# A gated mix of a spectral filter and an S5 state-space layer: FFT kept in SBUF, chunked recurrence kept in SBUF, transposes by DMA

## The chip, the cores and the metric

One Trainium2 chip, one core of it. The metric is the device time of one execution in microseconds (us). The engines are TensorE (PE, matmuls into PSUM; its weight loads are listed as PEld), VectorE (DVE), ScalarE (ACT), GpSimd (POOL) and SyncE (SP, which here only issues DMAs).

## What is computed

The input x has 2048 tokens of 1024 channels, in bf16. Two branches read it and a gate per token mixes them:

```python
def reference(A_x, A_w_r, A_w_i, B_x, ..., gate_w):
    x = A_x
    g = sigmoid((x * gate_w).sum(-1, keepdims=True))
    # A: real 2-D FFT over tokens and channels, times a filter, back
    X = rfft2(x.astype(float32)) * (A_w_r + 1j * A_w_i)     # 2048 x 513
    a = irfft2(X, s=(2048, 1024)).astype(bfloat16)
    # B: complex diagonal recurrence over the tokens, 1024 states
    Lam_bar = exp(dt * Lam);  B_bar = ((Lam_bar - 1) / Lam)[:, None] * (B_re + 1j * B_im)
    Bu = x @ B_bar.T
    for t in range(2048):
        h = Lam_bar * h + Bu[t]
    b = 2 * real(hs @ (C_re + 1j * C_im).T) + x * Dskip
    return g * a + (1 - g) * b
```

## The kernel before

**Start.** x is loaded by SP in 16 blocks of 128 tokens (L160) into the space that C will take later. PE transposes every block in 8 pieces of 128 x 128 against an identity (helper `pe_transpose_block`, L149; the copy out of PSUM is L150) to xT, channels on partitions. DVE forms the gate's sums (L165). A few dozen tiny operations on 128 x 8 tiles make the per-state constants.

**Spectral branch** (`gfnet`, a generator). The token index is split as 128 x 16 (16 times s1 plus s2). For every residue j: the channel DFT as 16 matmuls of 512 columns against a dense cosine and sine matrix (`fd`, L346), then the 128-point token DFT with twiddles (L358 to L361). The result goes to DRAM (L365) and is read back with tokens in another order, a corner turn (`s2w`, L446); a 16-point DFT over the residues follows (L452 to L455), the product with the filter W on DVE (L459 to L464), the inverse 128-point DFT (L476 to L479), a second turn through DRAM (L482, read back at L497), the inverse 16-point DFT (`is2`, L500 and L502, 256 columns each), and the inverse channel DFT (L518, 16 matmuls of 512 per block). ACT copies every result out of PSUM. The finished branch, times the gate, goes to DRAM (ga_scratch). Columns 0 and 512 of the spectrum are handled by a fix-up of small operations (`fixup`).

**Recurrence** (`pass1`, for each of 8 blocks of 128 states). B's block is loaded (L284) and transposed by PE. Tables of cosine and sine over 512 steps are made on ACT and DVE (L287 to L300, with the helper `sincos`, L226 to L235). Then for 4 chunks of 512 tokens: 16 matmuls (L309), copy to SBUF on ACT (L312), rotation into the frame that turns with the state (L314, L316, L318, bf16 on DVE), two real scans (L321), and the carry for the next chunk (L326 to L330). Chunk 0 is rotated back at once (`rotate_out`, L275 to L278); chunks 1 to 3 are stored to DRAM in the rotating frame (L337), and the tables as well.

**Order.** The main loop runs `pass1(jb)`, transposes two blocks of C, and pulls the spectral generator on by a budget of hand-given costs; the rest of the generator follows the last block. The framework's scheduler then orders the instructions of each engine: an instruction that is ready may be placed ahead of one that still waits for a buffer. A DMA belongs to the queue of the engine that issues it (SP for nearly all, POOL for the constants that are cast).

**Output.** The chunks are read back from DRAM (L562, and L547 for chunk 0), rotated back by DVE (L275 to L278), and for each of 16 token tiles 32 matmuls of 512 columns form the product with C (L580); DVE adds the skip term and the spectral branch (L588, L590, L593) and SP stores the tile (L595).

Of the kernel before, what the change touches and what calls it, by code (L numbers as in the profile page):

```python
# [19 lines left out]
S = 2048  # L20
D = 1024
K = 512
NP = 1024
# [3 lines left out]

MAGIC = 12582912.0
INV2PI = float(1.0 / (2.0 * np.pi))
CW1 = 6.28125  # L30
CW2 = float(2.0 * np.pi - 6.28125)
PI_LO = float(np.nextafter(np.float32(np.pi), np.float32(0.0)))
HALF_PI = float(np.pi / 2)

DEBUG = {}


def _host_consts():
    d = np.arange(D)[:, None]
    k = np.arange(K)[None, :]  # L40
    ang = 2 * np.pi * ((d * k) % D) / D
    G = np.zeros((D, 2 * K))
    G[:, :K] = np.cos(ang)
    G[:, K:] = -np.sin(ang)
    G[:, K] = (-1.0) ** np.arange(D)
    kk = np.arange(K)[:, None]
    n = np.arange(D)[None, :]
    angi = 2 * np.pi * ((kk * n) % D) / D
    ck = np.full((K, 1), 2.0)
    ck[0] = 1.0  # L50
    Ginv = np.zeros((2 * K, D))
    Ginv[:K, :] = ck * np.cos(angi)
    Ginv[K:, :] = -2.0 * np.sin(angi)
    Ginv[K, :] = (-1.0) ** np.arange(D)
    Ginv /= float(D * S)
    s1 = np.arange(P)[:, None, None]
    s2 = np.arange(16)[None, :, None]
    m1 = np.arange(P)[None, None, :]
    angT = 2 * np.pi * (((16 * s1 + s2) * m1) % S) / S
    Tc, Ts = np.cos(angT), np.sin(angT)  # L60
    p = np.arange(P)
    q = p // 8
    a = p % 8
    angK = 2 * np.pi * ((q[:, None] * q[None, :]) % 16) / 16
    delta = (a[:, None] == a[None, :]).astype(np.float64)
    Kc, Ks = delta * np.cos(angK), delta * np.sin(angK)
    J = np.zeros((P, P))
    J[np.arange(P), 127 - np.arange(P)] = 1.0
    P0 = np.zeros((P, P))
    P0[(128 - np.arange(P)) % 128, np.arange(P)] = 1.0  # L70
    f32 = lambda z: np.ascontiguousarray(z, dtype=np.float32)
    return dict(
        G=np.ascontiguousarray(G.astype(np.float32).astype(ml_dtypes.bfloat16)), Ginv=f32(Ginv),
        T3=f32(np.stack([Tc, Ts, -Ts], axis=0).transpose(2, 1, 0, 3)),
        K3=f32(np.stack([Kc, Ks, -Ks], axis=0)),
        R12=f32(np.stack([np.concatenate([Kc, Ks], 1), np.concatenate([-Ks, Kc], 1)], 0)),
        JP=f32(np.stack([J, P0], axis=0)),
    )
# [3 lines left out]
def kernel(  # L82
# [22 lines left out]
    cG = nc.inline_tensor(hc["G"], name="c_G").ap()  # L105
    cGinv = nc.inline_tensor(hc["Ginv"], name="c_Ginv").ap()
    cT3 = nc.inline_tensor(hc["T3"], name="c_T3").ap()
    cK3 = nc.inline_tensor(hc["K3"], name="c_K3").ap()
    cR12 = nc.inline_tensor(hc["R12"], name="c_R12").ap()
    cJP = nc.inline_tensor(hc["JP"], name="c_JP").ap()  # L110

    dram = ctx.enter_context(tc.tile_pool(name="dram", bufs=1, space=DRAM))
    ga_dram = dram.tile([S, D], BF16, name="ga_scratch")
    turn1_dram = dram.tile([16, P, 2, K], BF16, name="turn1_scratch")
    turn2_dram = dram.tile([16, P, 2, K], BF16, name="turn2_scratch")
    col0_dram = dram.tile([P, 16, 2], BF16, name="col0_scratch")
    h_dram = dram.tile([NCH, P, 8, 2, TC], BF16, name="h_scratch")
    tab2_dram = dram.tile([P, 8, 3, TC], BF16, name="tab2_scratch")
    g_dram = dram.tile([S], FP32, name="g_scratch")
    ccol_dram = dram.tile([P, 16, 2], BF16, name="ccol_scratch")  # L120

    cpool = ctx.enter_context(tc.tile_pool(name="cpool", bufs=1))
    xpool = ctx.enter_context(tc.tile_pool(name="xpool", bufs=1))
    ctpool = ctx.enter_context(tc.tile_pool(name="ctpool", bufs=1))
    h0p = ctx.enter_context(tc.tile_pool(name="h0p", bufs=1))

    actx = ExitStack()
    gconst = actx.enter_context(tc.tile_pool(name="gconst", bufs=1))
    gt = actx.enter_context(tc.tile_pool(name="gt", bufs=3))
    wp = actx.enter_context(tc.tile_pool(name="wp", bufs=3))  # L130
    wt = actx.enter_context(tc.tile_pool(name="wt", bufs=1))
    fx = actx.enter_context(tc.tile_pool(name="fx", bufs=1))
    p1 = actx.enter_context(tc.tile_pool(name="p1", bufs=2))
    p1t = actx.enter_context(tc.tile_pool(name="p1t", bufs=1))
    up = actx.enter_context(tc.tile_pool(name="up", bufs=3))
    rp = actx.enter_context(tc.tile_pool(name="rp", bufs=1))
    hp = actx.enter_context(tc.tile_pool(name="hp", bufs=3))
    cp = actx.enter_context(tc.tile_pool(name="cp", bufs=2))
    stg = actx.enter_context(tc.tile_pool(name="stg", bufs=3))
    psA = actx.enter_context(tc.tile_pool(name="psA", bufs=2, space=PSUM))  # L140
    psU = actx.enter_context(tc.tile_pool(name="psU", bufs=2, space=PSUM))

    ident = cpool.tile([P, P], BF16, name="ident")
    make_identity(nc, ident)

    def pe_transpose_block(src_ap, dst_ap, evac):
        pt = psU.tile([P, 8, P], BF16, name="pt", tag="psu")
        for j8 in range(8):
            nc.tensor.transpose(out=pt[:, j8, :], in_=src_ap[:, P * j8:P * (j8 + 1)], identity=ident)  # L149
        evac(out=dst_ap, in_=pt)  # L150

    CT = [ctpool.tile([P, 8, D], BF16, name=f"CT{ri}") for ri in range(2)]
    xT = xpool.tile([P, 8, S], BF16, name="xT")
    xT_A = xT.rearrange("p d (a b) -> p d b a", b=16)
    gw_bc = cpool.tile([P, D], BF16, name="gw_bc")
    nc.scalar.dma_start(out=gw_bc, in_=gate_w.partition_broadcast(P))
    glog = cpool.tile([P, 16], FP32, name="glog")
    for r in range(16):
        xn = CT[r // 8][:, r % 8, :]
        nc.sync.dma_start(out=xn, in_=x[P * r:P * (r + 1), :])  # L160
    for r in range(16):
        xn = CT[r // 8][:, r % 8, :]
        pe_transpose_block(xn, xT[:, :, P * r:P * (r + 1)], nc.vector.tensor_copy)
        gjunk = stg.tile([P, D], BF16, name="gjunk", tag="stg")
        nc.vector.scalar_tensor_tensor(out=gjunk, in0=xn, scalar=1.0, in1=gw_bc, op0=ALU.mult, op1=ALU.mult,  # L165
                                       accum_out=glog[:, r:r + 1])

    G_sb = gconst.tile([P, 8, 2 * K], BF16, name="G_sb", tag="G")
    cG_v = cG.rearrange("(j p) k -> p j k", p=P)
    for h in range(2):  # L170
        nc.sync.dma_start(out=G_sb[:, :, K * h:K * (h + 1)], in_=cG_v[:, :, K * h:K * (h + 1)])
    T3_sb = gconst.tile([P, 16, 3, P], BF16, name="T3_sb")
    nc.gpsimd.tensor_copy(out=T3_sb[:, 0, 0, 0:1], in_=xT[:, 7, S - 1:S])
    cT3_v = cT3.rearrange("j p t m -> p j t m")
    for q4 in range(4):
        nc.gpsimd.dma_start(out=T3_sb[:, 4 * q4:4 * (q4 + 1)], in_=cT3_v[:, 4 * q4:4 * (q4 + 1)])
# [162 lines left out]
    def gfnet():  # L339
# [13 lines left out]
        for j in range(16):  # L353
            X1 = X1_next
            if j + 1 < 16:
                X1_next = fd(j + 1)
# [269 lines left out]
```

## Time and profile before

| | |
|---|---|
| median of 3 runs (lowest to highest) | 517.84 us (516.38 to 517.95) |
| span of the profiled execution, first to last instruction | 515.2 us |
| what the median has beyond that span | 2.6 us |
| mean granted PE clock | 0.955 |
| busy ACT, share of the span | 211.2 us (41%) |
| DMA packets, bytes | 52751, 80.47 MB |
| HBM read, written | 55.68 MB, 28.34 MB |

The profile is of one execution. Its page gives busy time by engine, 40 equal slices of the span with the busy tenths of each engine, and groups of instructions by line (busy us, mean ns of one, idle time before them and what ended it). Matmuls are pipelined: a single record of 512 columns lasts 380 ns while the next starts some 217 ns later, so a group's busy time, and not the mean times the count, is what PE spent. Times of a view's first column are us from the span's start; the trace can also list who waited for whom, the work by stretch of time, and the instructions in order.

### The profile page before, as it was taken

The page shows a single profiled execution, that of the slowest core. Times are in us where ns is not written, and L with a number is a line of the kernel's source. Part 1 is how long each engine was busy: PE and PEld are TensorE (multiplying, and loading weights), DVE is VectorE, ACT ScalarE, POOL GpSimd, SP SyncE. Part 2 cuts the span into 40 slices and gives each one's busy share as a digit, 9 for nine tenths or more (in the row PEclk, how much of TensorE's full clock was granted, in tenths as well). Part 3 has the DMA queues.
Part 4 walks back from the last instruction along what each step waited for, and adds up shares of the span by engine and source line. Part 5 has one row for each costly group of instructions (what it writes and reads, how often), then busy time and mean ns, then how long its engine had stood idle before and what let it go on. Part 6 is the DMA issues. An engine that isn't in the chain of part 4 may idle for free. (4 is left out here: it accounts for less than half of the span.)

```text
span 515.2 us, 6351 instructions
## 1 busy us (share of the span) xinstructions
PE 444.0 (86%) x2343; PEld 225.7 (44%) x2343; DVE 351.3 (68%) x633; ACT 211.2 (41%) x278; POOL 14.0 (3%) x21
## 2 busy tenths in 40 slices
PE   1569988996999759999759999999977989999996
PEld 1546454553655314433425555545433433444442
DVE  4993794197129559999996504009695799999831
ACT  0018688735643725876828646444330000000000
POOL 6010000000001000000000000000000000000000
PEclk9979998998999879999988999999997997999999
DMA  8994343214212976488645335421586947542311
GB/s 213 261 239 89 114 143 113 92 38 157 83 41 84 225 200 199 155 268 256 214 106 184 125 107 173 141 83 43 193 328 230 368 139 262 168 129 87 117 42 41
DMA packets 52751, 80.47 MB, mean 156 GB/s; under 512 B 13680, under 2 KB 24176, under 8 KB 52080
## 3 DMA queue, kind: packets, MB, share of 16 engines
q1 hardware_dynamic: 47200, 75.82, 45.2%
q0 software_dynamic: 5328, 3.98, 5.9%
q8 instruction: 18, 0.29, 0.2%
q10 hardware_dynamic: 192, 0.27, 0.2%
q14 instruction: 13, 0.11, 0.1%
HBM read 55.68 MB, written 28.34 MB: 163 GB/s over the span
## 5 line engine op out<-in xcount | busy, mean ns | idle before, releaser
L309 PE MATMUL psu<-xT,BTs 128*128 128x512 bf16 x512 | 121.6, 384 | 1.3 <-ACT BTs L150 1.2
L314 DVE TENSOR_TENSOR cu<-u,tab 128x1024 bf16<-128x1024 bf16 x32 | 21.8, 681 | 86.1 <-ACT u L312 85.5
L580 PE MATMUL ps_y<-CT_124,hch 128*128 128x512 bf16 x192 | 74.4, 387 | 4.9 <-DVE hch L278 4.9
L309 PEld LDWEIGHTS <-BTs 128*128 128x128 bf16 x512 | 50.2, 99 | 60.7 <-issue 4.4
L580 PE MATMUL ps_y<-CT_125,hch 128*128 128x512 bf16 x192 | 74.3, 388 | 0.0
L346 PE MATMUL ps_fd<-G_sb,xT 128*128 128x512 bf16 x256 | 63.3, 403 | 8.8 <-ACT X_1131 L349 4.2
L580 PEld LDWEIGHTS <-hch 128*128 128x128 bf16 x384 | 37.8, 100 | 53.5 <-DVE hch L278 7.7
L321 DVE TENSOR_TENSOR_SCAN g<-r_sb,carry,v 128x512 bf16<-128x512 f32 x48 | 59.3, 1271 | 0.5
L518 PE MATMUL ps_id<-Ginv_sb,ZT 128*128 128x512 bf16 x256 | 57.7, 379 | 0.6 <-ACT ga L523 0.5
L312 ACT CAST u<-psu 128x1024 bf16<-128x1024 f32 x32 | 32.4, 1013 | 45.5 <-PE psu L309 42.6
L346 PEld LDWEIGHTS <-xT 128*128 128x128 bf16 x256 | 36.9, 147 | 31.7 <-issue 15.0
L518 PEld LDWEIGHTS <-ZT 128*128 128x128 bf16 x256 | 25.0, 98 | 30.9 <-issue 2.9
L593 DVE SCALAR_TENSOR_TENSOR o<-ps_y,omg,pre 128x1024 bf16<-128x1024 f32 x16 | 20.5, 1280 | 17.1 <-PE ps_y L580 17.1
L580 PE MATMUL ps_y<-CT_124,hch_3770 128*128 128x512 bf16 x64 | 25.5, 399 | 6.3 <-DMA hch_3770<-h_scratch 6.3
L523 ACT ACTIVATE ga<-ps_id,gA 128x1024 bf16<-128x1024 f32 x16 | 17.8, 1113 | 30.5 <-issue 21.0
L580 PE MATMUL ps_y<-CT_125,hch_3770 128*128 128x512 bf16 x64 | 25.3, 396 | 0.0
L580 PEld LDWEIGHTS <-hch_3770 128*128 128x128 bf16 x128 | 12.9, 102 | 22.8 <-DMA hch_3770<-h_scratch 6.5
L275 DVE TENSOR_TENSOR cu<-gch,tab_3804 128x1024 bf16<-128x1024 bf16 x24 | 16.4, 685 | 9.2 <-DMA gch<-h_scratch 9.0
L318 DVE TENSOR_TENSOR v<-cu,su 128x1024 bf16<-128x1024 bf16 x32 | 22.0, 688 | 0.4
L316 DVE TENSOR_TENSOR su<-u,tab 128x1024 bf16<-128x1024 bf16 x32 | 21.9, 685 | 0.0
L149 PE MATMUL pt<-ident,CT_124 128*128 128x128 bf16 x64 | 7.5, 311 | 15.5 <-DVE xT L150 9.4
L590 DVE SCALAR_TENSOR_TENSOR pre<-sk,omg,gac 128x1024 f32<-128x1024 bf16 x16 | 20.5, 1279 | 0.1
(661 smaller groups left out, 618.1 us busy)
## 6 DMA issues: line engine op xcount, KB each, us to landing
h_scratch<-g SPq DMA_DIRECT2D x24, 256.0 KB, 2.2
gch<-h_scratch SPq DMA_DIRECT2D x3, 2048.0 KB, 8.4
Bb<-turn_scratch SPq DMA_DIRECT2D x16, 256.0 KB, 3.4
Cq<-turn_scratch SPq DMA_DIRECT2D x16, 256.0 KB, 3.0
ga_scratch<-ga SPq DMA_DIRECT2D x16, 256.0 KB, 3.2
xc<-in_A_x_dram SPq DMA_DIRECT2D x16, 256.0 KB, 2.8
gac<-ga_scratch SPq DMA_DIRECT2D x16, 256.0 KB, 2.7
out_dram<-o SPq DMA_DIRECT2D x16, 256.0 KB, 2.0
```

The lines of the kernel that those rows point to most:

```text
L309: nc.tensor.matmul(psu[:, ri, :], lhsT=BTs[:, ri, dblk, :], rhs=xT[:, dblk, TC * c:TC * (c + 1)], start=(dblk == 0), stop=(dblk == 7))
L312: nc.scalar.copy(out=u, in_=psu)
L314: nc.vector.tensor_mul(out=cu, in0=u, in1=tab[:, 0:1, :].to_broadcast([P, 2, TC]))
L316: nc.vector.tensor_mul(out=su, in0=u[:, ::-1, :], in1=tab[:, 1:3, :])
L318: nc.vector.tensor_add(out=v, in0=cu, in1=su)
L321: nc.vector.tensor_tensor_scan(out=g[:, ri, :], data0=rb, data1=v[:, ri, :], initial=(0.0 if carry is None else carry[:, ri:ri + 1]), op0= ...
L346: nc.tensor.matmul(ps[:, K * h:K * (h + 1)], lhsT=xT_A[:, dblk, j, :], rhs=G_sb[:, dblk, K * h:K * (h + 1)], start=(dblk == 0), stop=(dblk ...
L518: nc.tensor.matmul(psy[:, 512 * nh:512 * (nh + 1)], lhsT=ZT[:, kc, c, :], rhs=Ginv_sb[:, 4 * c + kc, 512 * nh:512 * (nh + 1)], start=(i == ...
L523: nc.scalar.activation(out=ga, in_=psy, func=ACT.Copy, scale=gA[:, bp:bp + 1])
L580: nc.tensor.matmul(psy[:, 512 * dh:512 * (dh + 1)], lhsT=hch[:, jb, ri, P * tq:P * (tq + 1)], rhs=CT[ri][:, jb, 512 * dh:512 * (dh + 1)], ...
L590: nc.vector.scalar_tensor_tensor(out=pre, in0=sk, scalar=omg[:, tb:tb + 1], in1=gac, op0=ALU.mult, op1=ALU.add)
L593: nc.vector.scalar_tensor_tensor(out=o, in0=psy, scalar=omg[:, tb:tb + 1], in1=pre, op0=ALU.mult, op1=ALU.add)
```

## The change

The kernel is rewritten in all three parts; the outputs stay the same.

- **FFT.** x is loaded with the token split 128 x 16 on partitions (16 tokens of a partition are neighbours). DVE folds the channels by symmetry (sums and differences of d with d+512 and of d with its mirror), `fstage` does the 128-point real token DFT as the first matmul with the data as weights, so that channels come out on partitions (FX, in SBUF). For each of 16 groups of 128 frequencies, `fd` does the channel DFT on folded halves, `bf_w` the 16-point step and the product with W, `bi` the inverse 16-point step back into FX, again with the data as weights. `idm` and `fi` do the inverse channel and token DFT; the result goes to DRAM (ya_scratch) without the gate. The two DRAM turns, the fix-up and its small loads are gone. W is loaded by rows in group order (SP), the twiddle matrices by POOL, one load of 192 KB per group.
- **Recurrence.** Two blocks at a time (`ssm_pair`), chunk by chunk; tables are centred in the chunk and stay in SBUF, and the rotation back reads them in reversed order along the tokens. Magnitude and phase of the input factor go into ACT's scale and the tables' phase. Every chunk is rotated back at once, and h stays in SBUF.
- **Transposes.** B, x and C are transposed by `dma_start_transpose` on SP's queue (2-byte elements, DRAM to SBUF), not by PE. C takes the space of FX (`big`), so its transposes wait for the last `idm`.
- **Output.** C times h for a chunk runs beside the recurrence of a later chunk; the gate is computed per tile there, and the skip term is added on PE through an identity matmul.

The core of the new code (the constants' tables and the tiny setup left out):

```python
    def load_BT(jb):
        for ri, src in enumerate((B_B_re, B_B_im)):
            nc.sync.dma_start_transpose(out=BT[:, jb, ri], in_=src[P * jb:P * (jb + 1), :])
    def load_xT(c):
        for h in range(2):
            r0 = TC * c + 256 * h
            nc.sync.dma_start_transpose(out=xT[:, :, r0:r0 + 256], in_=x[r0:r0 + 256, :])
...
    def tables(q):                      # two blocks; frac() is three fp32 DVE operations on 1024
        ... 2 ACT on 512 (scale thp, bias beta), frac, 3 ACT Sin on 1024 ...
...
    def ssm_pair(c, q, hpool):
        ... 32 matmuls of 512 into psu; ACT copies each half to u with scale=rho ...
        nc.vector.tensor_mul(out=cu, in0=u, in1=tq[:, :, 0:1, :].to_broadcast(full))
        nc.vector.tensor_mul(out=su, in0=u[:, :, ::-1, :], in1=tq[:, :, 1:3, :])
        nc.vector.tensor_add(out=cu, in0=cu, in1=su)
        ... 4 scans of 512 into su, carry for the next chunk ...
        nc.vector.tensor_mul(out=cu, in0=su, in1=tq[:, :, 0:1, ::-1].to_broadcast(full))
        nc.vector.tensor_mul(out=u, in0=su[:, :, ::-1, :], in1=tq[:, :, 1:3, ::-1])
        nc.vector.tensor_add(out=h, in0=cu, in1=u)
...
    def fstage(jj):                     # 2 of 16 residues; eight DVE folds, the larger four on 512
        nc.vector.tensor_add(out=eo[:, :, 0, 1, 1:256], in0=xt[:, :, 511:256:-1], in1=xt[:, :, 1023:768:-1])
        ... for odd jj: 4 PSUM tiles, each 8 matmuls of 256 columns and
                nc.scalar.copy(out=FX[:, q + r, :, j0:j0 + 4], in_=ps[:, :, r, :].rearrange("p j c -> p c j")) for r in 0, 1
...
    def fd(g):      # weights FX[:, q, 8*g:8*g+8, :]; 1 matmul of 512 columns, 7 of 255 to 257; one ACT copy
    def bf_w(g):    # 8 matmuls of 256; two ACT copies into X (step 2); then
        nc.vector.tensor_mul(out=Y, in0=X, in1=W[:, 0:1, :].to_broadcast([P, 2, 514]))
        nc.vector.tensor_mul(out=t2, in0=X, in1=W[:, 1:2, :].to_broadcast([P, 2, 514]))
        nc.vector.tensor_sub(out=Y[:, 0, :], in0=Y[:, 0, :], in1=t2[:, 1, :])
        nc.vector.tensor_add(out=Y[:, 1, :], in0=Y[:, 1, :], in1=t2[:, 0, :])
    def bi(g):      # weights Y with step 2; 8 matmuls of 128 columns, 4 of 256; one ACT copy into FX
    def idm(j, yp): # weights FX[:, q, :, j] (step 16); 1 matmul of 512, 7 of 255 to 257; one ACT copy
    def fi(j, pm):  # 4 matmuls of 510 to 512; two ACT copies, one reversed; store to ya_scratch
...
    for jj in range(8):
        if jj + 3 < 8 and jj > 0:
            xts.append(load_x(jj + 3))
        for _ in fstage(jj):
            pass
        if jj == 1:
            load_BT(0)
        if jj == 3:
            load_BT(1)
    load_xT(0); tables(0); load_group(0); load_xT(1); load_group(1)
    for jb in range(2, 8):
        load_BT(jb)
    load_xT(2); load_xT(3)
    merge(Gen(fft_main()), Gen(ssm_first()), 80.0, 58.0)    # ssm_first: chunks 0 and 1
...
        for qd in range(4):
            for ri, src in enumerate((B_C_re, B_C_im)):
                nc.sync.dma_start_transpose(out=CT[:, :, ri, 256 * qd:256 * (qd + 1)], in_=src[256 * qd:256 * (qd + 1), :])
            nc.vector.tensor_scalar_mul(out=CT[:, :, 1, ...], in0=CT[:, :, 1, ...], scalar1=-1.0)
        def tile_out(tb):
            ... pr = xc * gate_w (DVE), sum on ACT, sigmoid on ACT, three tiny DVE operations,
            ... gac * g on ACT, xc * Dskip on DVE, 32 matmuls of 512 plus 2 with ident,
            nc.vector.scalar_tensor_tensor(out=xc, in0=psy, scalar=om, in1=gac, op0=ALU.mult, op1=ALU.add)
        bg = Gen(b_gen(2, h2))
        for _ in range(4):
            bg.step()
        merge(Gen(c_gen(0)), bg, 29.0, 24.0)
        merge(Gen(c_gen(1)), Gen(b_gen(3, hp)), 29.0, 29.0)
        run(c_gen(2))
        run(c_gen(3))
```

`merge` steps two generators so that their hand-given costs advance in the stated ratio. The pool `hp` of 8 buffers holds x's loads and folds first and h of chunks 0, 1 and 3 later. Removed with the old code: the PE transposes and their copies, the DRAM buffers for the turns, h, the tables and the gate, and the read-back of chunks 0 to 3.

More of the change, by code (lines that the diff above doesn't have):

```diff
@@ L29 @@
 INV2PI = float(1.0 / (2.0 * np.pi))
[L30 to L32 removed]
+TWO_PI_LO = 2.0 * float(np.nextafter(np.float32(np.pi), np.float32(0.0)))
 HALF_PI = float(np.pi / 2)
[L35 to L78 removed]
```

941 lines of the change are left out of this document (507 added, 434 removed).

## Prediction

> **What bounds the kernel now.** I read the page's busy shares and slices first, then busy time by stretch, then the waits, then the groups by line.
>
> ```profile
> span 515.2 us, 6351 instructions
> PE 444.0 (86%) x2343; PEld 225.7 (44%) x2343; DVE 351.3 (68%) x633; ACT 211.2 (41%) x278; POOL 14.0 (3%) x21
> ...
> PE   1569988996999759999759999999977989999996
> ...
> DVE  4993794197129559999996504009695799999831
> ```
>
> TensorE (PE) is busy for 444.0 of 515.2 us and idle for 71. DVE is second, and its row of slices shows full stretches and empty ones. By stretch (columns: length, then busy us of PE, weight load, DVE, ACT and POOL, then clock, DMA share, GB/s):
>
> ```profile
> 220.00:240.00 20.00, 18.76 (x81) 7.55 (x80) 20.00 (x51) 14.79 (x17) 0.00 (x0) 1.00 0.80 245
> 320.00:340.00 20.00, 19.49 (x111) 10.50 (x111) 0.00 (x1) 10.43 (x12) 0.00 (x0) 1.00 0.46 151
> 400.00:420.00 20.00, 20.00 (x95) 9.08 (x93) 17.93 (x24) 0.00 (x0) 0.00 (x0) 1.00 0.74 274
> ```
>
> At 220 DVE is full, at 320 it idles through the inverse FFT while PE is full. The waits name DVE's loss and the DRAM turns that the change removes:
>
> ```profile
> DVE cu L314 <- ACT u L312: 85.5, 7, 27.1
> PE ps_y L580 <- DMA hch_3770<-h_scratch: 6.3, 1, 6.3
> PE ps_is_2408 L500 <- DMA Cq<-turn_scratch: 6.1, 1, 6.1
> PE ps_s_1542 L452 <- DMA Bb<-turn_scratch: 5.7, 1, 5.7
> ```
>
> PE loses 18.1 us on the three turns through DRAM; DVE loses 85.5 us because recurrence work is not spread under the FFT. So PE's amount of work bounds the kernel, and DVE would be the next bound.
>
> **PE after the change.** Prices first:
>
> ```profile
> 487.29 23.28 PE ps_y L580 x107
> ...
> 301.82 0.27 PE L500 MATMUL ps_is_2828<-R_sb,Cq 128*128 128x256 bf16 x1
> 301.93 0.27 PE L502 MATMUL ps_is_2828<-R_sb,Cq 128*128 128x256 bf16 x1
> ...
> L149 PE MATMUL pt<-ident,bn 128*128 128x128 bf16 x128 | 10.3, 223 | 0.9 <-DMA bn<-in_B_B_im_dram 0.5 <-ACT CT_124 L150 0.3
> ...
> L346 PE MATMUL ps_fd<-G_sb,xT 128*128 128x512 bf16 x256 | 63.3, 403 | 8.8 <-ACT X_1131 L349 4.2 <-ACT X_782 L349 2.3 <-DVE xT L150 1.5
> ...
> L518 PE MATMUL ps_id<-Ginv_sb,ZT 128*128 128x512 bf16 x256 | 57.7, 379 | 0.6 <-ACT ga L523 0.5
> ...
> L346 PEld LDWEIGHTS <-xT 128*128 128x128 bf16 x256 | 36.9, 147 | 31.7 <-issue 15.0 <-DVE xT L150 1.6
> ```
>
> A 512-column matmul costs 23.28/107 = 0.218 us, a 256-column one 0.11 (start to start), a 128-column one 10.3/128 = 0.08. The old FFT: 63.3 + 57.7, plus 192 of 512 columns in the three middle stages (41.8) and 128 of 256 (14.1) = 177 us; the transposes are 384 x 0.08 = 31. The new FFT, from the loops of the diff: fstage 128 x 0.11 = 14.1; fd 16 x (0.218 + 7 x 0.11) = 15.8; bf_w 128 x 0.11 = 14.1; bi 16 x (8 x 0.08 + 4 x 0.11) = 17.3; idm is like fd, but its weights step 16 elements, and such a load takes 147 ns, longer than a 256-column matmul covers: 16 x (0.218 + 7 x 0.147) = 20.0; fi 64 x 0.218 = 13.9. Sum 95. Recurrence and output projection keep 512 matmuls each (111 each); the skip term adds 32 identity matmuls, 7. PE falls to about 325 us.
>
> **DVE after the change.**
>
> ```profile
> 238.09 0.68 DVE L277 TENSOR_TENSOR su<-g,tab 128x1024 bf16<-128x1024 bf16 x1
> 238.69 0.42 DVE L459 TENSOR_TENSOR t_2247<-Wr_b,X_2244 128x512 bf16<-128x512 bf16 x1
> 239.03 0.42 DVE L460 TENSOR_TENSOR t_2249<-Wi_b,X_2244 128x512 bf16<-128x512 bf16 x1
> ...
> L321 DVE TENSOR_TENSOR_SCAN g<-r_sb,carry,v 128x512 bf16<-128x512 f32 x48 | 59.3, 1271 | 0.5
> ...
> L593 DVE SCALAR_TENSOR_TENSOR o<-ps_y,omg,pre 128x1024 bf16<-128x1024 f32 x16 | 20.5, 1280 | 17.1 <-PE ps_y L580 17.1
> ...
> L230 DVE SCALAR_TENSOR_TENSOR ang<-rot_kk,ang 128x512 f32<-128x512 f32 x8 | 5.5, 689 | 0.2
> ...
> L231 DVE TENSOR_SCALAR ang<-ang 128x512 f32<-128x512 f32 x8 | 3.4, 424 | 0.2
> ```
>
> Start to start, 1024 bf16 elements cost 0.60 us and 512 cost 0.34; carried on, 2048 cost 1.13. A scan costs 59.3/48 = 1.24. One ssm_pair (two blocks, one chunk): six operations of 2048 (6.8, 0.2 more for the two that wait for the one before), four scans 4.9, carries 0.4 = 12.3 us; sixteen of them 197, almost what the old recurrence cost. Besides: bf_w 2.0 x 16 = 32 (two of 1028, two of 514); pm 1.2 x 8 = 10; tables, with fp32 rows doubled, 2.4 x 4 = 10 against some 30 before; fstage 1.9 x 8 = 15; tile_out 2 x 0.60 + 1.2 + three tiny = 2.8 x 16 = 45; C's sign 5; setup 7. Sum about 320: no gain of note for DVE. DVE and PE are now level, so the time comes from how the stages fit.
>
> **ACT** evacuates every PSUM tile:
>
> ```profile
> L312 ACT CAST u<-psu 128x1024 bf16<-128x1024 f32 x32 | 32.4, 1013 | 45.5 <-PE psu L309 42.6 <-issue 2.9
> L293 ACT CAST tab<-sn_f 128x512 bf16<-128x512 f32 x8 | 5.0, 623 | 0.0
> ```
>
> 1.0 us per 1024 and 0.62 per 512 elements make some 200 us, the same as now. It sets the pace only in fstage: four pairs x 8 copies x 0.62 = 20 us. Strided FX writes could cost more; bounds 0 and double (20 us), and I take 0, since these rows are the nearest.
>
> **DMA transposes** are the unknown; the trace has none. Bounds per 256 KB:
>
> ```profile
> 0.75 7.35 SPq L160 DMA_DIRECT2D CT_124<-in_A_x_dram  x8
> ...
> q1 hardware_dynamic: 47200, 75.82, 45.2%
> q0 software_dynamic: 5328, 3.98, 5.9%
> ```
>
> Below: plain loads of 256 KB are taken at 7.35/8 = 0.92 us each. Above: q1's packets take 0.452 x 16 x 515.2/47200 = 79 ns, whatever they hold (q0's, half as large, 91); if a transpose moves 256-byte pieces, 256 KB are 1024 packets, 64 per engine, 5.1 us. I take 1.3 us: the source rows are the same 2-KB rows as the plain loads', plus 40% for the scattered write. The Trainium skill ("DMA: Bandwidth & Descriptors", Latency and other measured facts) gives 261 GB/s, about 1.0 us, which would take some 14 us off the sum; no run here shows it.
>
> **The stages, summed.** *Fold and forward token DFT:* x in 16 units x 0.92 = 14.7, the B transposes queued between them 4 x 1.3 = 5.2, start and landing 6, then the last pair's fold (1.9) and eight copies (5.0): 33 us. *First FFT results* for DVE: 5. *Wait for W:* the SP queue carries x (14.7), all 32 units of B and x transposes (41.6), two W groups (2) and landing (4) before the third group's W: 62 us; DVE gets there at 33 + 5 + 4 (two groups) + 11 (most of a pair) = 53. Wait 9; none at 0.92. Behind that product in DVE's order stand the next pair's rotations; ACT then finds no free u, and PE no free PSUM. *FFT beside chunks 0 and 1:* DVE 8 x 12.3 + 32 + 10 + 7 = 147, PE 81 + 55.7 = 137; so level a pair leaves gaps, 7%: 158. *C:* its 16 units start only when FX is free, 20.8 + landing 4, while PE has some 16 us of other work: 9; behind the waiting matmul on PE stand chunk 2's, for which ACT and DVE wait. *Output of chunk 0 beside the rest of chunk 2:* PE 4 x 7.45 + 3 x 6.96 = 51; *of chunk 1 beside chunk 3:* DVE 4 x 2.8 + 4 x 12 = 59; 5% on both: 53 + 62. *Chunks 2 and 3:* PE alone, 8 x 7.45 = 60. *Tail:* 3, the final evacuation and store. 33 + 5 + 9 + 158 + 9 + 53 + 62 + 60 + 3 = 392 us of span; the median of the runs (517.84) lies 2.6 above the profile's span, so **395 us**. The waits on DRAM turns (18 us) are gone in this sum; what is late instead is DVE in the first two thirds and W or C behind the transposes. MM's 16 loads move to the POOL queue, 192 KB each against about 9 us per group, so I cost them at nothing; without that cover they would hold bf_w. The gate moves into tile_out as a chain DVE, ACT, ACT, DVE, ACT (some 3.5 us a tile by the rows above); I cost it at its DVE share only, because a tile's matmuls cover 7.45 us and two tiles are in flight; uncovered, it would add up to 16 x 3.5 = 56 us, but only if both buffers ran dry each time.
>
> **Rivals.**
>
> *A: the reversed reads lose the fast mode.* The return rotation reads its tables backwards along the innermost axis ([::-1]), the fold reads x so too; no DVE row here does.
>
> ```profile
> L165 DVE SCALAR_TENSOR_TENSOR gjunk<-CT_125,gw_bc 128x1024 bf16<-128x1024 bf16 x8 | 9.7, 1215 | 0.0
> ```
>
> That is 1024 bf16 elements at one per cycle, 0.53 us over the 0.68 above. Two of six operations per pair: +2.1 x 16 = 34, +4 in the fold, almost all where DVE bounds: 432 us. The Trainium skill ("Advanced Engine Details and Errata", VectorE Performance Modes) lists a unit step of +1 or -1 as allowed, which speaks against this rival; no run here shows it. Chance 0.20.
>
> *B: the last x loads fall behind the transposes.* x's last two loads need a buffer that the fold frees; the transposes need none. The scheduler pulls ready loads ahead of blocked ones:
>
> ```profile
> 29.73 0.64 SPq L448 DMA_DIRECT2D Wr_b<-in_A_w_r_dram  x1
> ...
> 36.85 0.33 SPq L284 DMA_DIRECT2D bn<-in_B_B_re_dram  x1
> ```
>
> Here W, far later in the program, was issued before B. Then the fold ends at about 62 + 7 us, 36 later, and swallows the wait of 9: 395 + 36 - 9 = 422 us. Chance 0.15.
>
> *C, slower than before: transposes run packet by packet.* At 5.1 us per 256 KB the third W comes at 14.7 + 163 + 6 = 184, a wait of 131 in place of 9, and C at 82 + 4 - 16 = 70 in place of 9: 395 + 122 + 61 = 578 us. Each microsecond over 1.3 costs 32 + 16 = 48 us, so it turns slower than before at 1.3 + 123/48 = 3.9 us per 256 KB (68 GB/s). For it speaks that q0's smaller packets cost no less than q1's; against, that a fixed price is unlikely from 1.6-KB means alone. The Trainium skill ("VectorE: DVE Perf Modes", The three transpose paths) gives 1309 ns for a 128x128 block by DMA: 10.5 us per 256 KB, by which the sum would be about 835 us; no run here shows it. Chance 0.06.
>
> **Numbers.** Forecast 0.55, A 0.20, B 0.15, C 0.06, better than all of them 0.04. The runs lie within 0.3% of their median, so 0.3% is the limit of no change. Low end: no wait for W (-9), C hidden (-9), no gaps (-11, -5), fold 29 (-4): 357. High end: A together with half of B's delay or transposes at 1.8 us, 432 + 23 = 455. Faster 0.93, same 0.01, slower 0.06.
>
> **What would show it.** Right: PE busy near 325-335, DVE 310-330, ssm table products backwards at the duration of those forwards, gaps of PE behind the C transposes under 15 us. A: backward products near 2.2 us. B: fold's last x landing after 50 us. C: transposes landing over 4 us per 256 KB, DVE waiting on W. Wrong altogether: PE over 360 us through weight loads, or ACT full in the FFT.

## The result, and the profile after

The changed kernel takes 406.1 us (median of 4 runs, 404.0 to 408.1) where the kernel before takes 517.9 on the same chip (516.4 to 518.9): a ratio of 0.785, 95% interval 0.781 to 0.789. The forecast was 395 us with a range of 357 to 455. Below, differences between kernels are differences of such ratios times 517.9 us; each ratio is uncertain by 0.002 to 0.004, so a difference between two kernels is uncertain by 2 to 3 us.

The page of the profile after (span, busy time, then three rows of 40 slices of 10 us each):

```profile
span 402.1 us, 4944 instructions
PE 336.1 (84%) x1794; PEld 176.0 (44%) x1827; DVE 304.4 (76%) x492; ACT 199.7 (50%) x273; POOL 12.9 (3%) x31
...
PE   0668965888878889799889698999999986979995
...
DVE  0882380999899999998948897499897987953351
...
PEclk9999987999999999999999899999999999689999
```

PE's work fell by 108 us (444.0 to 336.1) and the span by 113; its idle time stayed, 71 before, 66 now. By this balance the gain is matmul work that is gone (products of the FFT, 384 transposes), and the DRAM waits that went were replaced by others. The balance rests on two profiles; no run took matmul work alone out of either kernel. The dips of PE's clock (8 7, then 8, then 6 8) stand where its own row dips: about 50 to 70, 220 and 340 us.

Against the stages of the forecast (ends in us from the start, from the instructions in order):

| stage | forecast end | measured end | what was measured |
|---|---|---|---|
| forward token DFT | 33 | 41.5 | last copy into FX |
| first product with W | 38 | 45.8 | its start |
| wait for the third W | 62 | 70.8 | 10.1 us long, forecast 9 |
| FFT beside chunks 0 and 1 | 205 | 209.9 | last copy of a result |
| output of chunk 0 | 267 | 263.9 | fourth final combination |
| output of chunk 1 | 329 | 335.1 | eighth |
| chunks 2 and 3 | 389 | 398.7 | sixteenth |
| end | 392 | 402.1 | span |

The wait for W. SP's queue in order (start, time, and what it issues), then waits of the whole run (total us, times, longest):

```profile
6.24 3.26 SPq L208 DMA_TRANSPOSE BT<-in_B_B_re_dram  x1
...
38.25 1.31 SPq L208 DMA_TRANSPOSE BT<-in_B_B_re_dram  x1
...
56.48 10.56 SPq L213 DMA_TRANSPOSE xT<-in_A_x_dram  x4
67.14 0.81 SPq L425 DMA_DIRECT2D W<-in_A_w_r_dram  x1
```

```profile
DVE Y L478 <- DMA W<-in_A_w_r_dram: 10.1, 1, 10.1
PE ps_xe L464 <- DMA MM<-c_MM: 14.8, 14, 4.1
...
DVE pr L650 <- DMA xc<-in_A_x_dram: 34.8, 11, 5.5
PE psy L672 <- DVE xc L662: 13.3, 5, 3.9
```

From 38 us on, most transposes of 256 KB occupy the queue for 1.31 us, which is the 1.3 that was taken. Beside the first loads of x, the first four took 12.3 us in all, and all the transposes ahead of the third W took 50.5 instead of 41.6. It is issued behind the last of them at 67.14, and DVE gets it at 70.75 (the sum had it landing at 62). The MM waits of PE were costed at nothing, and the two last lines, the load of x for an output tile, were not in the sum at all.

The reversed reads, from the groups (total us, mean ns): L343 reads the table forwards, L363 the same shape backwards.

```profile
L343 DVE TENSOR_TENSOR cu<-u,tab 128x2048 bf16<-128x2048 bf16 x16 | 19.5, 1217 | 8.9 <-ACT u L336 8.9
L363 DVE TENSOR_TENSOR cu<-su,tab 128x2048 bf16<-128x2048 bf16 x16 | 19.5, 1217 | 0.0
```

### The profile page after: what moved, and what is told of

Same layout as the page of the kernel before. It is cut to its first block, busy times and chain, and to the rows that moved or that the text cites. A ratio compares the mean times of both kernels' runs of the same rounds, so it can differ in the third digit from the quotient of the medians.

```text
span 402.1 us, 4944 instructions
## 1 busy us (share of the span) xinstructions
PE 336.1 (84%) x1794; PEld 176.0 (44%) x1827; DVE 304.4 (76%) x492; ACT 199.7 (50%) x273; POOL 12.9 (3%) x31
## 4 chain that ended last, share of the span: by engine, by line
issue 30%; DVE 30%; PE 23%; DMA 9%; ACT 2%; SPq 2%; POOL 1%; DVEq 0%; POOLq 0%; ACTq 0%
PE psy L669 15%; DVE su L349 10%; PE psu L332 6%; DMA xc<-in_A_x_dram 3%; DMA MM<-c_MM 3%; DVE xc L675 2%; DVE u L364 2%; SPq L639 2%; DVE cu L345 2%; DMA out_dram<-xc 2%; DVE cu L363 2%; DVE h L365 2%; DVE su L344 1%; DMA big<-in_B_C_im_dram 1%; PE psy L672 1%
## 5 line engine op out<-in xcount | busy, mean ns | idle before, releaser
L669 PE MATMUL psy<-big,h 128*128 128x512 bf16 x500 | 120.4, 391 | 1.9 <-DVE xc L675 0.7
L332 PE MATMUL psu<-xT,BT 128*128 128x512 bf16 x491 | 120.7, 385 | 1.1 <-issue 0.2
L669 PEld LDWEIGHTS <-h 128*128 128x128 bf16 x512 | 51.4, 101 | 80.4 <-issue 23.1
L332 PEld LDWEIGHTS <-BT 128*128 128x128 bf16 x512 | 50.8, 99 | 52.5 <-issue 3.0
L349 DVE TENSOR_TENSOR_SCAN su<-r_sb,carry,cu 128x512 bf16<-128x512 f32 x48 | 58.3, 1264 | 0.1
L336 ACT ACTIVATE u<-psu,rho 128x1024 bf16<-128x1024 f32 x32 | 35.7, 1116 | 31.6 <-PE psu L332 31.6
L343 DVE TENSOR_TENSOR cu<-u,tab 128x2048 bf16<-128x2048 bf16 x16 | 19.5, 1217 | 8.9 <-ACT u L336 8.9
L675 DVE SCALAR_TENSOR_TENSOR xc<-psy,om,gac 128x1024 bf16<-128x1024 f32 x16 | 20.4, 1274 | 5.4 <-PE psy L672 5.4
L672 PE MATMUL psy<-xc,ident 128*128 128x512 bf16 x32 | 12.6, 398 | 13.3 <-DVE xc L662 13.3
L503 ACT CAST big<-ps_q 128x1024 bf16<-128x1024 f32 x16 | 16.2, 1011 | 12.3 <-PE ps_q L502 12.2
L345 DVE TENSOR_TENSOR cu<-cu,su 128x2048 bf16<-128x2048 bf16 x16 | 19.5, 1222 | 0.3
L365 DVE TENSOR_TENSOR h<-cu,u 128x2048 bf16<-128x2048 bf16 x16 | 19.5, 1219 | 0.1
L363 DVE TENSOR_TENSOR cu<-su,tab 128x2048 bf16<-128x2048 bf16 x16 | 19.5, 1217 | 0.0
L364 DVE TENSOR_TENSOR u<-su,tab 128x2048 bf16<-128x2048 bf16 x16 | 19.5, 1216 | 0.0
L344 DVE TENSOR_TENSOR su<-u,tab 128x2048 bf16<-128x2048 bf16 x16 | 19.5, 1216 | 0.0
```

The source lines that it names most:

```text
L332: nc.tensor.matmul(psu[:, ri, :], lhsT=BT[:, jb, ri, dblk, :], rhs=xT[:, dblk, TC * c:TC * (c + 1)], start=(dblk == 0), stop=(dblk == 7))
L336: nc.scalar.activation(out=u[:, jj], in_=psu, func=ACT.Copy, scale=rho[:, jb:jb + 1])
L343: nc.vector.tensor_mul(out=cu, in0=u, in1=tq[:, :, 0:1, :].to_broadcast(full))
L344: nc.vector.tensor_mul(out=su, in0=u[:, :, ::-1, :], in1=tq[:, :, 1:3, :])
L345: nc.vector.tensor_add(out=cu, in0=cu, in1=su)
L349: nc.vector.tensor_tensor_scan(out=su[:, jj, ri, :], data0=r_sb[:, jb:jb + 1].to_broadcast([P, TC]), data1=cu[:, jj, ri, :], initial=(0.0 ...
```

## The experiments

Two questions were left by the profile: what each of the waits for W, MM, C and x is worth, and whether DVE's sum bounds the stage beside the FFT, as the forecast had it (DVE 147 us, PE 137, and 7% for gaps).

**1 to 3: W and MM, each alone and both.** In the first, W of the groups 2 to 15 is loaded by POOL:

```diff
+        eng = nc.sync if g < 2 else nc.gpsimd
-            nc.sync.dma_start(out=w[0:64, ri, 0:513], in_=sv[:, 4 * g:4 * g + 4, :])
+            eng.dma_start(out=w[0:64, ri, 0:513], in_=sv[:, 4 * g:4 * g + 4, :])
...
         WT[g] = w
+        m = fr.tile([P, 6, P], BF16, name="MM")
+        nc.gpsimd.dma_start(out=m, in_=cMM[g])
```

The last two lines stood ahead of W before: the edit also puts MM's load behind W's on POOL's queue.

> W of groups 2 to 15 is loaded from the POOL queue, so it no longer stands behind the B and x transposes on SP; nothing else is changed. Theory (the W wait is on the path): in the trace of the changed kernel DVE stands 10.1 us at 60.7 for the third W, and from 80 us on it is busy 19 of 20 us, so a loss ahead of that is never made up; the time falls by 8 to 12 us, to 394 to 398, and DVE's wait for W goes. Rival (something else comes last there: PE's waits for MM, 4 to 5 us in each of the groups 2 and 3, or the first products of the recurrence, whose x and B come by the same transposes): the time falls by 0 to 4 us, to 402 to 406, and DVE waits at the same place for ACT or PE.

Measured: 402.2 us, ratio 0.777 (0.773 to 0.780), 4.2 us less. DVE's wait for W is gone, and PE waits longer for MM in its place, up to 7.1 us at a time:

```profile
PE ps_xe L465 <- DMA MM<-c_MM: 16.4, 13, 7.1
```

The gain is at the upper edge of the rival's range, and DVE waits 6.5 us at the same place for ACT, as the rival has it: more than half of the 10 us came back at the next wait. Part of that is the edit's own doing: a load of MM took 9.3 us from issue to landing among W's loads there, where the two of that stretch (45 to 60 us) took 6.2 at most in the changed kernel. In the second, the twiddle matrices are two tiles, the forward half with three buffers and loaded behind `bf_w`:

```diff
+        m = mfp.tile([P, 3, P], BF16, name="MF")       # mfp: bufs=3
+        nc.gpsimd.dma_start(out=m, in_=cMM[g][:, 0:3, :])
...
         Ys[g] = Y
+        if g + 3 < 16:
+            load_MF(g + 3)
```

> MM is split in two halves; the half for the forward step has three buffers and is loaded one group earlier, as soon as the forward step of three groups before has read it. PE's 14 waits for MM (14.8 us in all) should go. Theory (costed at nothing is right: DVE bounds the stage, and in the first groups the third W is later still): the time changes by less than 3 us, 403 to 407, and the idle time of PE moves to waits for DVE. Rival (MM holds the forward step of each group, about 1 us in 14 groups, on the path): the time falls by 8 to 15 us, to 391 to 398.

Measured: 408.8 us, ratio 0.791 (0.788 to 0.793), 3 us more, little beyond the uncertainty. PE's waits for MM are gone, and PE stands 12.2 us for the product with W instead (which waits for W itself, 9.8 us), followed by slow matmuls (PE's instructions in order; in brackets the idle time before):

```profile
74.83 0.29 PE L506 MATMUL ps_q<-MI,Y 128*128 128x128 bf16 x1 [12.19 <-DVE Y L490]
```

> W on the POOL queue and the split MM together. Theory (each alone leaves the other wait in the groups 2 and 3, from group 4 on DVE bounds): 12 to 16 us less, 390 to 394, more than the sum of the two alone. Rival (only W counts): the same as with W alone, within 2 us.

Measured: 398.5 us, ratio 0.770 (0.767 to 0.772), 7.9 us less than the changed kernel. Alone -4 and +3, together -8: the two waits stand at the same place, one behind the other, and with the split MM its forward half no longer stands behind W's loads. The theory's 12 to 16 was too much.

**4: the store in the way of the next load.**

```diff
-            nc.vector.scalar_tensor_tensor(out=xc, in0=psy, scalar=om, in1=gac, op0=ALU.mult, op1=ALU.add)
-            nc.sync.dma_start(out=out2[P * tb:P * (tb + 1), :], in_=xc)
+            nc.vector.scalar_tensor_tensor(out=gac, in0=psy, scalar=om, in1=gac, op0=ALU.mult, op1=ALU.add)
+            nc.sync.dma_start(out=out2[P * tb:P * (tb + 1), :], in_=gac)
```

> The final combination is written over gac instead of over xc and stored from there, so the load of x for the tile after next waits for the skip term's matmul alone and not for the store. Theory (the turn evacuation, store, load, product with the gate weights stands in PE's way from 320 to 360 us, 8 us idle and the slower clock behind it): 6 to 11 us less, 395 to 400, and PE's waits for the skip term (13.3 us, 5 times) fall below 5 us. Rival (the gate chain or DVE's scans hold the tile, the loads are only late beside them): less than 2 us, 404 to 408, and the waits move to another line.

Measured: 403.2 us, ratio 0.780 (0.777 to 0.782), 2.7 us less, little more than the uncertainty. From the first to the last final combination its profiled execution takes 154.8 us where the changed kernel takes 160.8, so the stage gains the 6 us of the theory there: 1.9 before the fourth, nothing from the fourth to the eighth (71.4 against 71.2), 4.3 behind the eighth. But the first comes at 241.5 instead of 236.7; C's transposes were slower in that execution. PE's wait for the skip term fell from 13.3 to 8.0, not under 5.

**5 and 11: does DVE bound the stage beside the FFT?**

```diff
+        if c < 2:
+            nc.vector.tensor_mul(out=h, in0=su, in1=tq[:, :, 0:1, ::-1].to_broadcast(full))
+        else: ...  # all three operations
```

> Leaves out, for chunks 0 and 1, the second product and the sum of the return rotation (8 pairs, two operations of 1.22 us each: 19.5 us less work of DVE beside the FFT); h of these chunks is then half of what it should be. Theory (DVE bounds the stage beside the FFT, as 19 to 20 of 20 us in the stretches from 80 to 180 say, and PE, 16 to 18 of 20 there, is close behind): the last product with W, at 157.0 in the changed kernel, comes 9 to 13 us earlier and the whole is 7 to 12 us shorter. Rival 1 (PE's order and its waits for MM bound the stage): less than 4 us. Rival 2 (DVE alone bounds): 18 us or more.

Measured: 409.5 us, ratio 0.789 (0.787 to 0.791): no shorter. DVE's work from 80 to 120 us falls, PE's hardly moves. By stretch (length, busy PE, PEld, DVE, ACT, POOL, then clock, DMA share, GB/s), the changed kernel and then this one:

```profile
80.00:120.00 40.00, 33.36 (x234) 20.50 (x238) 38.51 (x55) 29.54 (x36) 3.22 (x6) 1.00 0.26 70
```

```profile
80.00:120.00 40.00, 34.94 (x234) 21.55 (x238) 34.69 (x51) 28.79 (x35) 3.22 (x6) 0.96 0.26 68
```

The last product with W ends at 156.3 instead of 157.4. An engine that is busy 38.5 of 40 us was not the bound. Since PE still waited for MM there, the omission was tried once more on top of experiment 3:

> The kernel with W on the POOL queue and the split MM (398.5 us), with the second product and the sum of chunks 0 and 1's return rotation left out as well (19.5 us of DVE; h of these chunks is half of what it should be). Leaving them out alone brought nothing, and the split MM alone brought nothing. Theory (PE's waits and DVE's work bound this stage together, each just below the other; both must go): the last product with W, at 150.6 without the omission, comes at 138 to 144, and the whole is 6 to 12 us under 398.5. Rival (PE's own work and its turns with ACT bound the stage whatever DVE does): the last product at 148 or later, the whole at 396 or more.

Measured: 400.6 us, ratio 0.772 (0.767 to 0.776), within the uncertainty of experiment 3 without the omission. The last product with W starts at 147.9 against 150.6. Both theories about sums fall, and the rivals' numbers come out: 19.5 us of DVE work are worth less than the uncertainty there. From 70 to 155 us, PE is busy 74.5 us with and without the omission, at a mean clock of 0.92 with it and 0.96 without, while DVE's busy time falls from 79.3 to 71.8. DVE's instructions in order, then PE's, then 1-us stretches of this kernel show one turn of the queues:

```profile
79.13 2.43 DVE L349 TENSOR_TENSOR_SCAN su<-r_sb,carry,cu 128x512 bf16<-128x512 f32 x2
81.49 0.40 DVE L494 TENSOR_TENSOR Y<-Y,t 128x514 bf16<-128x514 bf16 x1
```

```profile
81.94 0.23 PE L510 MATMUL ps_q<-MI,Y 128*128 128x128 bf16 x1 [2.22 <-DVE Y L494]
...
84.43 0.31 PE L510 MATMUL ps_q<-MI,Y 128*128 128x128 bf16 x1
84.54 0.31 PE L511 MATMUL ps_q<-MI,Y 128*128 128x128 bf16 x1
...
89.19 0.22 PE L510 MATMUL ps_q<-MI,Y 128*128 128x128 bf16 x1
89.24 0.22 PE L511 MATMUL ps_q<-MI,Y 128*128 128x128 bf16 x1
```

```profile
80.00:81.00 1.00, 0.00 (x0) 0.00 (x0) 1.00 (x2) 0.00 (x0) 0.98 (x2) 1.00 0.37 75
...
84.00:85.00 1.00, 1.00 (x9) 0.89 (x8) 1.00 (x3) 0.57 (x1) 0.00 (x0) 0.50 0.00 0
...
87.00:88.00 1.00, 1.00 (x8) 0.68 (x7) 0.79 (x3) 1.00 (x2) 1.00 (x3) 1.00 0.09 28
```

The last step of the product with W (Y) sits in DVE's queue behind the pair's scans. PE stands 2.2 us for it, and then runs at half clock for some 3 us: products of 128 columns start 0.11 us apart at 84.4 and 0.05 at 89.2. Meanwhile DVE has work of its own; a few us later it stands 3.4 us for ACT. PE's products for the next X are done at 87.6, but in ACT's queue three sine tables stand ahead of its copy (ACT's instructions, then DVE's):

```profile
87.45 1.06 ACT L318 ACTIVATE tab<-xa 128x1024 bf16<-128x1024 f32 x1
...
90.39 0.73 ACT L488 CAST X<-ps_xo 128x512 bf16<-128x512 f32 x1
...
91.15 0.70 DVE L492 TENSOR_TENSOR Y<-X,W 128x1028 bf16<-128x1028 bf16 x1 [3.36 <-ACT X L488]
```

From 70 to 155 us DVE waits 11.0 us for these copies where experiment 3 has 2.9, and PE waits 8.4 us for DVE's Y where it has 8.0. So the engines hold each other up in turn, and what is taken from DVE's work comes back as DVE's wait. That the order in the queues of DVE and ACT is the cause is read from the traces; a kernel with the product ahead of the scans, or the copy ahead of the tables, was not tried.

**6: C by PE instead of DMA.**

```diff
+        for db in range(8):
+            cn = h2.tile([P, 2, D], BF16, name="cn", tag="h")
+            ... 2 plain loads of 256 KB, 16 PE transposes into one PSUM tile, 2 ACT copies (scale -1 for the imaginary half)
```

> Undoes one part: C is loaded plainly (natural rows, 16 loads of 256 KB into the buffers of chunk 2's h) and transposed by PE against the identity, 128 transposes of 0.08 us = 10 us of PE; ACT evacuates them in 16 copies of 1 us, the sign of the imaginary half among them, so DVE's 2.8 us for the sign go. Theory (the DMA transposes are the cheaper way although PE loses about 7 us behind them between 200 and 240): 3 to 10 us longer, 409 to 416, PE busy 346. Rival (the stage is bound by the transposes on the DMA queues, whose 8 pieces take 24 us with DMA at over 100%, while PE and ACT have idle time for the work): 3 to 8 us shorter.

Measured: 431.8 us, ratio 0.833 (0.829 to 0.836), 25 us more. The plain loads are issued only at 215, behind the last store of the FFT's results, where the changed kernel issues its first transpose at 198.9; PE waits 10 us for them, and its transposes stand ahead of chunk 2's products in its queue; the first product with C comes at 229.8 instead of 210.8. So this undo is 25 us the worse way; how much of that is its late start, which comes with where its buffers lie, and how much the transposes on PE is not separated.

**7: plain loads in place of all transposes.**

> Every DMA transpose (B, x, C) is replaced by a plain load of the same bytes to the same tile, in pieces of 2 KB for B and 512 bytes for x and C, so the products have wrong operands. It prices the transposing alone. Theory (transposes cost about 1.3 us per 256 KB against 0.9 for plain loads, so the third W is issued some 10 us earlier and C lands earlier): 5 to 12 us shorter, the wait for W under 3 us, the load of x for the first tile issued before 215. Rival (the bytes are the cost, transposing costs nothing): within 3 us of the changed kernel.

Measured: 394.5 us, ratio 0.761 (0.759 to 0.763), 12 us less. The third W is issued at 46.2 instead of 67.1, the FFT ends 8.3 us earlier, and from there to the first final combination it takes 22.1 us instead of 27.4 (the x load for the first tile is issued at 207.5). So transposing costs 12 us over plain loads of the same bytes in these pieces; the rival, that the bytes are the cost, is out.

**8 to 10: C's stretch, from 199 to 237 us.** First, x and the FFT's result for the first two tiles go by POOL:

```diff
-            nc.sync.dma_start(out=xc, in_=x[P * tb:P * (tb + 1), :])
+            (nc.gpsimd if tb < 2 else nc.sync).dma_start(out=xc, in_=x[P * tb:P * (tb + 1), :])
...
```

> The loads of x and of the FFT's result for the first two tiles of the output go by the POOL queue, so they no longer stand behind C's transposes on SP. Theory (the first tile's gate product at 227.2 and PE's wait of 3.9 us for its skip term come from that queue): 3 to 6 us shorter, and the first final combination at 230 to 233 instead of 236.7. Rival (the buffers come free no earlier, or the last piece of C, which lands at the same time, is what PE then waits for): less than 1.5 us.

Measured: 420.9 us, ratio 0.811 (0.806 to 0.815), 13 us more; the opposite of the theory. SP's queue, and the DMA issues (KB each, median us from issue to landing):

```profile
222.27 10.69 SPq L639 DMA_TRANSPOSE big<-in_B_C_im_dram  x1
```

```profile
xc<-in_A_x_dram POOLq DMA_DIRECT2D x2, 256.0 KB, 11.6
gac<-ya_scratch POOLq DMA_DIRECT2D x2, 256.0 KB, 15.8
xc<-in_A_x_dram SPq DMA_DIRECT2D x2, 256.0 KB, 2.6
```

Beside the transposes, a load of x by POOL takes 11.6 us; by SP, without transposes beside it, it takes 2.6, and POOL's loads of MM (192 KB) take 2.9 in the median of the changed kernel, so the queue alone is not the cause. The last transpose holds SP for 10.7 us where it took 3.0. For these four loads, queueing behind the transposes was the cheaper order. Then half of C is transposed early:

```diff
+        for qd in range(4):                            # behind the last pair of chunk 1
+            cs = slice(256 * qd, 256 * (qd + 1))
+            nc.sync.dma_start_transpose(out=xT[:, :, cs], in_=B_C_re[cs, :])
...
-                                         rhs=CT[:, jb, ri, ds], start=(i == 0), stop=False)
+                                         rhs=CTs[ri][:, jb, ds], start=(i == 0), stop=False)
```

> The real half of C is transposed into the columns of x's transpose that chunks 0 and 1 no longer need, issued behind the last pair of chunk 1 and so beside the inverse FFT; only the imaginary half still waits for the FFT's buffer. Same transposes, half of them earlier. Theory (from the last FFT result at 209 to the first final combination at 236.7 the DMA queue's 24 us of transposes set the pace, and the x loads queue behind them): that stretch falls from 27 to 13 to 17 us and the whole by 8 to 13 us, to 393 to 398. Rival (the early transposes hold up the stores of the FFT's results on the same queue, so the FFT ends later by as much as C comes earlier): within 3 us of 406.

Measured: 406.9 us, ratio 0.785 (0.781 to 0.789): no difference. The mechanism worked: the first final combination comes at 230.1 instead of 236.7, and the x load at 213 instead of 223. But the third comes at 250.0 (251.0 before), the eighth at 336.5 (333.9): PE's waits (total us, times, longest, from 200 us on) now name the turn of a PSUM tile, L678 being the final combination:

```profile
PE psy L675 <- DVE xc L665: 9.4, 5, 3.7
PE psy L672 <- DVE xc L678: 7.4, 2, 5.5
```

So neither theory as stated: the FFT was not held up (its end moved by 0.8 us), the gain was lost later, in the output stage: from the fourth to the eighth final combination it takes 75.4 us, and 71 to 73 in every other trace from the changed kernel on. And the two broadcast loads:

```diff
-        nc.gpsimd.dma_start(out=gw_bc, in_=gate_w.partition_broadcast(P))
+        nc.sync.dma_start(out=gw_bc, in_=gate_w.partition_broadcast(P))   # both loads, behind C's loop
...
```

> The two broadcast loads (gate weights and skip weights, 256 KB each) that go by the POOL queue at 214, in the middle of C's transposes, go by SP behind them. Theory (two queues at once slow the transposes: beside these loads a 512-KB piece took 3.0 to 4.2 us on SP, and with four more loads there 6.9 and 10.7 us, against 1.8 to 2.6 without): the last piece of C is issued 3 to 5 us earlier, the whole is 2 to 5 us shorter. Rival (the DMA engines' bandwidth is simply shared, bytes for bytes): the sum of the loads is the same, within 1.5 us of the changed kernel.

Measured: 410.6 us, ratio 0.793 (0.789 to 0.796), 4 us more. C's pieces take 23.9 us from the first to the end of the last, 24.4 in the changed kernel: two loads more or less hardly change the transposes, which speaks for the rival's bytes, but its time missed too, as x now lands behind two more loads (PE waits 7.9 us for the skip term, at one place). In experiment 8 the four extra loads cost more than their bytes, here two do not; a threshold was not looked for.

**12: the three edits that can be joined.**

> Three edits together: W on the POOL queue with the split MM (398.5 us alone), the final combination over gac (403.2 alone), and C's real half transposed early (406.9 alone). Theory (PE and DVE are level in every stage, so time freed at one place is lost again at the next wait: the early C brought the first final combination 6.5 us forward and PE then lost as much from 320 to 360, waiting for x and for the combination; with that wait eased, too, the gain is kept): 389 to 395 us, the first final combination at 222 to 227, PE's idle time from 200 to the end under 14 us. Rival (DVE's recurrence of the chunks 2 and 3 alone paces the output stage, so its end does not move with its start): 396 to 401, no better than the first edit alone.

Measured: 396.0 us, ratio 0.767 (0.764 to 0.770), 9.3 us less than the changed kernel. Against experiment 3 alone (0.767 to 0.772) the intervals overlap, so the other two edits are not shown to add in the whole. The profiled execution of it was faster than its other runs (span 389.0, mean clock 0.986), with the first final combination at 223.9 as in the theory; the median is at the rival's edge. It is, with experiment 3, the best version found that keeps the whole computation, 23% under the kernel before.

## Why the prediction was right, point by point

- **What bounds.** Right by the balance of the two profiles: PE's work fell by 108 us and the span by 113. That it is the cause is argued, as no run changed PE's work alone. PE came to 336 where 325 was forecast; the prices were those of the full clock, which was not granted all the time. DVE 304, forecast 320 (C's sign 2.8 instead of 5; the rest was not broken down).
- **Fold and token DFT, 33 us.** Too short by 8.5, the largest single error. The fold itself ended at 29.2 (28 in the sum). The step "eight copies (5.0)" failed: at 29.2 ACT had not eight but 14 of its 32 copies (L399) to make, some 7 us, and the first tables' operations with a table load (L311 to L319) lay between them, some 5 us. The sum put the copies on ACT and forgot the tables there, though they are in the same part of the code.

```profile
30.00 2.09 ACT L399 CAST big<-ps_f 128x512 bf16<-128x512 f32 x4
32.29 1.28 ACT L318 ACT_TABLE_LOAD   x1 [0.20 <-DVE xa L248]
33.58 1.06 ACT L318 ACTIVATE tab<-xa 128x1024 bf16<-128x1024 f32 x1
```

- **Wait for W, 9.** Right in place and cause; the length (10.1) is in part luck. W came 8.8 us later than summed, as the transposes took 50.5 us instead of 41.6 (the 1.3 each was a choice between wide bounds, and its meeting 1.31 later in the queue is luck as well), and DVE came 7.7 later (60.7 instead of 53), as the fold was late. And its worth is not its length: taking it away gave 4.2 us, as the wait for MM came next.
- **MM at nothing.** Right alone (the split MM gave none), and the named condition, "without that cover they would hold bf_w", holds as soon as W comes early: the pair is worth 8.
- **FFT beside chunks 0 and 1, 158.** The end was right within 5 us, the reason was not. "DVE 147, PE 137, level, 7% gaps" says that less DVE work would shorten it to PE's 137; 19.5 us less did nothing. As far as the traces show, the stage's length comes from the order in the engines' queues and from what a pause of PE costs after it; no run reordered them.
- **C, 9, and the output of chunk 0, 53.** The two together took 54.0 instead of 62. From the FFT's end to the first final combination the trace has 27 us, but chunk 2's products covered much of it. And less was done: of chunk 2's 16 scans only eight were done by 263.9, where the sum had all of them.
- **Output of chunk 1, 62.** 71.2, and it is the same work: the recurrence that slid out of the stage before ran here, 20 scans instead of 16, five pairs instead of four. By the sum's own prices, 4 x 2.8 + 5 x 12 = 71. C and the two outputs together took 125.2 us instead of 124. The load of x is not the cause: PE waits 1.9 us for a skip term in this stage, and with experiment 4 it takes 71.4. The scans by stage (length, busy DVE, clock, DMA share, GB/s; one that lies across the border counts in both), then all engines in this stage, in the changed kernel and in experiment 4:

```profile
209.90:263.90 54.00, 10.08 (x9) 0.97 0.51 132
263.90:335.10 71.20, 23.95 (x20) 1.00 0.14 45
```

```profile
263.90:335.10 71.20, 68.38 (x312) 30.97 (x317) 65.98 (x80) 20.36 (x26) 0.00 (x0) 1.00 0.14 45
```

```profile
266.80:338.20 71.40, 69.11 (x320) 31.14 (x319) 66.66 (x79) 18.91 (x25) 0.00 (x0) 1.00 0.14 45
```

- **The last two chunks, 60.** 63.6, at a mean clock of 0.92. Here the term was mis-sized: "two tiles are in flight" covered the gate chain, but not the load ahead of it, which waited for the store of two tiles before. Experiment 4 took 59.3.
- **Rival A** (reversed reads): 1217 ns both ways, no loss. The Trainium skill's rule ("Advanced Engine Details and Errata", VectorE Performance Modes), that a unit step backwards keeps the mode, agrees.
- **Rival B** (last x loads behind the transposes): the last x load was issued at 21.13, ahead of x's own transposes; the fold ended at 29.
- **Rival C** (packet by packet): 1.31 us per 256 KB against the 3.9 of its break-even; only beside x's loads did single ones come near that (3.3 to 3.9). The stream ran at 262144 B / 1.31 us = 200 GB/s. By estimate, the Trainium skill's 1309 ns per 128x128 block ("VectorE: DVE Perf Modes", The three transpose paths) would be 10.5 us, and its 261 GB/s ("DMA: Bandwidth & Descriptors", Latency and other measured facts) would be 1.0; the trace agrees with neither.

Stage by stage the errors are +8.5 (fold), -4 (FFT), -8 and +9 (C with chunk 0, then chunk 1: one piece of work that changed stages), +4 (the last two chunks) and under 1 for the rest; the 10 us between 392 and the span are what they leave after cancelling in part.

## What to carry to other kernels

Price a wait by what is late next at the same place, and take away both at once: here -4 and +3 made -8. An engine busy 96% of a stretch is no proof that it bounds it; look at what stands in its queue ahead of the operation that the other engine waits for. When a stage comes out longer than forecast, count the work done in it before looking for a wait: here a recurrence pair had moved from one stage to the next. Try both orders for ordinary loads and a run of DMA transposes: four loads beside it cost 13 us, two moved behind it cost 4.

## What was not expected of the hardware

**A pause of PE can be paid twice.** In the changed kernel, PE's instructions in order and 1-us stretches:

```profile
335.19 3.61 PE L669 MATMUL psy<-big,h 128*128 128x512 bf16 x15 [0.68 <-DVE xc L675]
342.30 0.59 PE L672 MATMUL psy<-xc,ident 128*128 128x512 bf16 x1 [3.50 <-DVE xc L662]
342.68 6.18 PE L669 MATMUL psy<-big,h 128*128 128x512 bf16 x16
348.69 0.38 PE L672 MATMUL psy<-xc,ident 128*128 128x512 bf16 x1
348.90 3.40 PE L669 MATMUL psy<-big,h 128*128 128x512 bf16 x15
```

```profile
340.00:341.00 1.00, 0.00 (x0) 0.00 (x0) 1.00 (x2) 0.46 (x1) 0.00 (x0) 1.00 0.00 0
...
345.00:346.00 1.00, 1.00 (x4) 0.30 (x2) 1.00 (x2) 0.00 (x0) 0.00 (x0) 0.50 0.00 0
...
348.00:349.00 1.00, 1.00 (x6) 0.48 (x5) 1.00 (x2) 0.00 (x0) 0.00 (x0) 1.00 0.00 0
```

In the pause of 3.5 us the granted clock falls to 0.50, where it stays until 347.8, and sixteen products take 6.2 us instead of 3.6. In every 1-us stretch looked at the clock is full or half, but for those in which it changes; a mean of 0.97 over 402 us is, by estimate, 24 us at half clock, pauses included. The Trainium skill ("TensorE: Matmul & The Clock Gate", Part 1: The HAM clock gate) tells of the two states and of a freely running window of about 3.4 us, an idle one of which halves the clock; the traces agree on the states. On the length they do not: pauses of 2.2 and 2.4 us were followed by half clock (experiments 11 and 4), one of 3.27 us in experiment 4 was not:

```profile
338.33 5.30 PE L669 MATMUL psy<-big,h 128*128 128x512 bf16 x16 [2.40 <-DVE gac L675]
...
350.79 3.61 PE L669 MATMUL psy<-big,h 128*128 128x512 bf16 x16 [3.27 <-DVE gac L675]
```

**Transposes and loads of another queue slow each other** beyond what their bytes ask for when four loads of 256 KB come beside them: 11.6 us instead of 2.6 to land, with 10.7 instead of 3.0 us for the transpose (experiment 8). The last two pieces of C took 17.6 us instead of 7.2; the 1 MB of the four loads would be 5 us by the stream's 200 GB/s, an estimate.
